# Starting the first values half an exponential early, and the row-sum count as a full-width product, in a fused attention and SwiGLU kernel

## The chip, the cores and the metric

The kernel runs on one core of one Trainium2 chip. The metric is the device time of one execution in microseconds (us), of the slowest core, here the only one.

Short names: PE is TensorE with its products, PEld its loads of weights, ACT is ScalarE, DVE is VectorE, POOL is GpSimd, SP is SyncE, which only issues transfers. L487 is line 487 of the kernel in question; the changed kernel's lines are 3 higher from the first edit on.

## The reference, cut to what matters

```python
# x [1, 2048, 640], 32 heads of 192, caches of 2048 keys, F = 1536, all bf16
xn = _layernorm(x)
q = (xn @ wq) per head                       # [32, 2048, 192]
scores = q @ k_cache.T * (192 ** -0.5)
p = softmax(scores);  o = p @ v_cache
s = o (heads joined) @ wo
g = silu(silu(xn @ w1) * (xn @ w3) @ w2)
return x + s * g
```

## The kernel before

The attention is a stream of 1024 steps (head h, block of 512 queries qb, pair of key tiles p). A step n has three pieces: *scores n* (six products into a PSUM tile `st2`, of which there are two), *exponential n* on ACT (into `pT2`, which frees the score tile), *values n* (16 products that read `pT2`). On PE, scores run two steps ahead of values. The exponential takes no maximum; instead the kernel keeps the reciprocals of the row sums and at the end counts the rows in which these are in range. If the count is not full, an exact attention is run; with these inputs it never is. `project` and `project0` make the queries from the normalised rows `xnT` and `xnS`, a copy with the halves exchanged; `P` is 128.

```python
def emit_scores(h, qb, p):
    st2 = ps_st.tile([P, 1024], F32, tag="st2", name="st2")     # two buffers
    # rounds: pairs of products, rows 0-63 into columns 0:512, rows 64-127 into 512:1024
    # [cut: the first two steps have two full-height products in place of two rounds]
    for r, (ka, qa, kb, qb2) in enumerate(rounds):
        nc.tensor.matmul(st2[:, 0:512], lhsT=ka, rhs=qa, ...)
        nc.tensor.matmul(st2[:, 512:1024], lhsT=kb, rhs=qb2, ...)
    pT2 = pp.tile([P, 1024], BF16, tag="pT2", name="pT2")
    nc.scalar.activation(out=pT2[:], in_=st2[:], func=ACT.Exp, scale=att_scale)
    return pT2

# [cut: head_start(): loads, layernorm of the first 512 rows, scores(0), scores(1)]

for n, (h, qb, p) in enumerate(stream):
    # [cut: project(h + 1, qb) or ffn_open(qb) at p == 0]
    if h == 0 and qb == 0 and p == 3:
        project(1, 0)
    if h == 0 and qb + 1 < NQB and p == (5 if qb == 0 else 4):
        project0(qb + 1)
    scores(n + 2)
    values(n)
    # [cut: end of a block, SwiGLU pieces, layernorm of later rows: first_head()]
```

`project(1, 0)` makes head 1's queries for the first 512 rows. It uses the two row halves of the array at the same time, and the products that pair with the other half read `xnS`, a copy of the normalised rows `xnT` with the halves exchanged. That copy is made by two transfers that SP issues at about 11 and 12 us. `project0(1)` makes head 0's queries for rows 512 to 1023, and half of these rows reach `xnT` by two transposing transfers (`ln_turn_dma`), which SP issues at about 18 to 20 us. `P` is 128; `DC` is 5, the 640 columns of x in pieces of 128.

```python
def swap_halves(g):
    nc.sync.dma_start(out=xnS[0:64, :, qs], in_=xnT[64:P, :, qs])
    nc.sync.dma_start(out=xnS[64:P, :, qs], in_=xnT[0:64, :, qs])

def ln_turn_dma(g, i):
    nc.sync.dma_start_transpose(out=xnT[:, :, q0:q0 + P], in_=xns.pop((g, i))[:])

def two_products(W, qs):                       # of project(h, qb)
    for j in range(2 * DC):
        for r in range(2):
            rows = slice(r * 64, (r + 1) * 64)
            xs = xnT if j % 2 == r else xnS
            nc.tensor.matmul(ps[:, r * 512:(r + 1) * 512], lhsT=W[rows, j, :], rhs=xs[rows, j // 2, qs], ...)

def project0(qb):
    for half in range(2):
        for c in range(DC):
            nc.tensor.matmul(ps[:, half * 512:(half + 1) * 512], lhsT=W[:, half * DC + c, :], rhs=xnT[:, c, qs], ...)
```

The count stands in the output stage, after the fifth of 16 output tiles (24 products each):

```python
    if i == 4:
        cnt = ps_st.tile([P, 1024], F32, tag="st2", name="cnt")
        nc.tensor.matmul(cnt[0:2, 0:2], lhsT=ones[:], rhs=okb[:], start=True, stop=True)   # ones: [P, 2]
```

Of the kernel before, what the change touches and what calls it, by code (L numbers as in the profile page):

```python
# [8 lines left out]
ACT = mybir.ActivationFunctionType  # L9
ALU = mybir.AluOpType  # L10
AX = mybir.AxisListType
BF16 = mybir.dt.bfloat16
# [3 lines left out]
P = 128  # L16
# [112 lines left out]
def _kernel_impl(  # L129
# [12 lines left out]
    nc = tc.nc  # L142
# [16 lines left out]
    att_scale = float(DH) ** -0.5  # L159
# [243 lines left out]
    def project0(qb):  # L403
        W = loads[0]["W"]
        qAB, qC = q_tiles(0, qb)
        qs = slice(qb * 512, (qb + 1) * 512)
        ps = ps_st.tile([P, 1024], F32, tag="st2", name="ps0")
        for half in range(2):
            for c in range(DC):
                nc.tensor.matmul(ps[:, half * 512:(half + 1) * 512], lhsT=W[:, half * DC + c, :], rhs=xnT[:, c, qs],  # L410
                                 start=(c == 0), stop=(c == DC - 1))
        cast_pair(qAB, ps)
        nc.vector.tensor_copy(out=qC[64:P, 0, :], in_=qAB[0][0:64, :])
        nc.vector.tensor_copy(out=qC[0:64, 0, :], in_=qAB[0][64:P, :])
        nc.vector.tensor_copy(out=qC[0:64, 1, :], in_=qAB[1][64:P, :])
# [18 lines left out]
    def project(h, qb):  # L434
        qAB, qC = q_tiles(h, qb)
        cast_pair(qAB, two_products(loads[h]["W"], slice(qb * 512, (qb + 1) * 512)))
        move_q(qAB, qC, 0)
        move_q(qAB, qC, 1)
# [3 lines left out]
    def ffn_open(qb):  # L442

        pairs[qb] = [qp.tile([P, 512], BF16, tag=t, name=t) for t in ("qA", "qB")]
        cast_pair(pairs[qb], two_products(wrest["wf"], slice(qb * 512, (qb + 1) * 512)))
# [9 lines left out]
    def swiglu(h, qb):  # L455

        m = h // 2
        qs = slice(qb * 512, (qb + 1) * 512)
        z = qtiles[h, qb][0][1][0:PGW, :]
        r0 = (m % 2) * PGW  # L460
        hid = hT[r0:r0 + PGW, m // 2, qs]
        if h % 2 == 0:
            t = hbp.tile([P, 512], BF16, tag="pt", name="pt")
            nc.scalar.activation(out=t[0:PGW, :], in_=z, func=ACT.Tanh, scale=0.5)  # L464
            nc.vector.scalar_tensor_tensor(out=hid, in0=t[0:PGW, :], scalar=1.0, in1=z, op0=ALU.add, op1=ALU.mult)  # L465
        else:
            nc.vector.scalar_tensor_tensor(out=hid, in0=hid, scalar=0.5, in1=z, op0=ALU.mult, op1=ALU.mult)
# [3 lines left out]
    def emit_scores(h, qb, p):  # L471


        KW = loads[h]["KW"]
        (qA, qB), qC = qtiles[h, qb]
        ks = slice(p * P, (p + 1) * P)
        st2 = ps_st.tile([P, 1024], F32, tag="st2", name="st2")
        rounds = [(KW[0:64, 0, ks], qA[0:64, :], KW[64:P, 1, ks], qC[64:P, 0, :]),
                  (KW[0:64, 3, ks], qC[0:64, 0, :], KW[64:P, 4, ks], qA[64:P, :]),
                  (KW[0:64, 1, ks], qC[0:64, 1, :], KW[64:P, 2, ks], qB[64:P, :])]  # L480
        if (h, qb) == (0, 0) and p < 2:
            rounds = rounds[2:]
            nc.tensor.matmul(st2[:, 0:512], lhsT=KW[:, 0, ks], rhs=qA[:], start=True, stop=False)
            nc.tensor.matmul(st2[:, 512:1024], lhsT=KW[:, 4, ks], rhs=qA[:], start=True, stop=False)
        nr = len(rounds)
        for r, (ka, qa, kb, qb2) in enumerate(rounds):
            nc.tensor.matmul(st2[:, 0:512], lhsT=ka, rhs=qa, start=r == 0 and nr == 3, stop=r == nr - 1)  # L487
            nc.tensor.matmul(st2[:, 512:1024], lhsT=kb, rhs=qb2, start=r == 0 and nr == 3, stop=r == nr - 1)  # L488
        pT2 = pp.tile([P, 1024], BF16, tag="pT2", name="pT2")
        nc.scalar.activation(out=pT2[:], in_=st2[:], func=ACT.Exp, scale=att_scale)  # L490
        return pT2

    exps = {}
# [5 lines left out]
    def scores(n):  # L499
        if n < len(stream):  # L500
            exps[n] = emit_scores(*stream[n])

    def values(n):

        h, qb, p = stream[n]
        if p == 0:
            for r in range(2):
                obanks[r] = ps_o.tile([P, 1024], F32, tag=f"ob{r}", name=f"obank{r}")
        vt = loads[h]["vt"]
        pT2 = exps.pop(n)  # L510
        for t in range(2):
            for j in range(4):
                start = p == 0 and t == 0 and j % 2 == 0
                stop = p == NPAIR - 1 and t == 1 and j % 2 == 1
                for r in range(2):
                    nc.tensor.matmul(obanks[r][:, j * 256:j * 256 + DH + 1],  # L516
                                     lhsT=pT2[r * 64:(r + 1) * 64, t * 512 + j * P:t * 512 + (j + 1) * P],
                                     rhs=vt[r * 64:(r + 1) * 64, 2 * p + t, 0:DH + 1], start=start, stop=stop)
        if p < NPAIR - 1:
            return  # L520
        if h % HG == 0 and qb == 0:
            ostages[0] = stp.tile([P, NQT, HG * DH], BF16, tag="ostage", name="ostage")
        ov = [obanks[r][:].rearrange("p (j w) -> p j w", j=4)[:, :, 0:DH + 1] for r in range(2)]
        osum = osp.tile([P, 4, DH + 1], F32, tag="osum", name="osum")
        nc.vector.tensor_copy(out=osum[:], in_=ov[0])  # L525
        nc.vector.tensor_tensor(out=osum[:], in0=osum[:], in1=ov[1], op=ALU.add)  # L526
        osums[0] = osum
# [96 lines left out]
    def finish_block(n):  # L624
        h, qb, _ = stream[n]
        finish_values(h, qb)
        loads_after(h, qb)
# [26 lines left out]
    for n, (h, qb, p) in enumerate(stream):  # L654
        if p == 0 and n > 0:
            if h + 1 < H:
                project(h + 1, qb)
            else:
                ffn_open(qb)
        if h == 0 and qb == 0 and p == 3:  # L660
            project(1, 0)
        if h == 0 and qb + 1 < NQB and p == (5 if qb == 0 else 4):
            project0(qb + 1)
        scores(n + 2)
        values(n)
        if p == 0 and n > 0:
            finish_block(n - 1)
        if p == (5 if h == 0 else 2) and h < 2 * NPIG:
            swiglu(h, qb)
        if p == 4 and h + 1 == H:  # L670
            ffn_close(qb)
        if h == 0:
            first_head(qb, p)
# [6 lines left out]
    fsb = main.enter_context(tc.tile_pool(name="fsb", bufs=2))  # L680
# [15 lines left out]
    for qb in range(NQB):  # L696
        qs = slice(qb * 512, (qb + 1) * 512)
        for fl in range(FL2 // P):
            ps = pools[(qb * (FL2 // P) + fl) % 2].tile([P, 1024], F32, tag="st2", name="ps_gu")
            for r, w in enumerate((wrest["w1"], wrest["w3"])):  # L700
                for c in range(DC):
                    nc.tensor.matmul(ps[:, r * 512:(r + 1) * 512], lhsT=w[:, c, fl * P:(fl + 1) * P], rhs=xnT[:, c, qs],  # L702
                                     start=(c == 0), stop=(c == DC - 1))
# [10 lines left out]
    okb = fsb.tile([P, 2], BF16, tag="okb", name="okb")  # L714
    nc.vector.tensor_scalar(out=okb[:, 0:1], in0=ends[:, 0:1], scalar1=RL_MAX, scalar2=None, op0=ALU.is_lt)
    nc.vector.tensor_scalar(out=okb[:, 1:2], in0=ends[:, 1:2], scalar1=RL_MIN, scalar2=None, op0=ALU.is_gt)
    ones = fsb.tile([P, 2], BF16, tag="ones", name="ones")
    nc.vector.memset(ones[:], 1.0)


    def g_of(i):
        return hT[:, 0:DC, i * P:(i + 1) * P]

    for i in range(NQT):
        ps = pools[i % 2].tile([P, 1024], F32, tag="st2", name="ps_f")
        for fc in range(FC):
            for b, (c0, c1) in enumerate(DP):
                nc.tensor.matmul(ps[:, b * 512:b * 512 + c1 - c0], lhsT=hT[:, fc, i * P:(i + 1) * P],  # L728
                                 rhs=w2_sb[:, fc, c0:c1], start=(fc == 0), stop=(fc == FC - 1))
        for b, (c0, c1) in enumerate(DP):  # L730
            t = fsb.tile([P, 512], BF16, tag="ft", name="ft")
            pv = ps[:, b * 512:b * 512 + c1 - c0]
            nc.scalar.activation(out=t[:, 0:c1 - c0], in_=pv, func=ACT.Tanh, scale=0.5)
            nc.vector.scalar_tensor_tensor(out=g_of(i)[:, c0 // P:c1 // P, :],
                                           in0=t[:, 0:c1 - c0].rearrange("p (a w) -> p a w", w=P), scalar=1.0,
                                           in1=pv.rearrange("p (a w) -> p a w", w=P), op0=ALU.add, op1=ALU.mult)
        if i == 4:
            cnt = ps_st.tile([P, 1024], F32, tag="st2", name="cnt")
            nc.tensor.matmul(cnt[0:2, 0:2], lhsT=ones[:], rhs=okb[:], start=True, stop=True)
            tot = fsb.tile([1, 1], F32, tag="tot", name="tot")  # L740
            nc.vector.tensor_reduce(out=tot[:], in_=cnt[0:1, 0:2], axis=AX.X, op=ALU.add)
            nc.vector.tensor_copy(out=flag[:], in_=tot[:])
# [65 lines left out]
```

## Time and profile before

| | before |
|---|---|
| time, median of the first 3 runs | 1939.36 us (1938.64 to 1939.67) |
| span of the profiled run | 1936.7 us |
| PE busy | 1927.1 us |
| PE busy between 16.10 and 1660 us | 1643.64 of 1643.90 us |

The head of the profile page of the kernel before, and its chain of waits (what released the last work, followed back from the end):

```profile
PE 1927.1 (100%) x27273; PEld 1317.2 (68%) x27281; DVE 654.4 (34%) x997; ACT 1181.5 (61%) x1278; POOL 282.1 (15%) x501
...
PE 99%; DVE 0%; DMA 0%; ACT 0%; issue 0%
```

PE is busy all the time and nearly the whole chain is PE. So a change is worth something only if it takes work or a wait off PE. The list of PE's waits (line and tile, what it waited for, us in total, times, longest):

```profile
PE pk L569 <- POOL ident_bf masks.py:199: 2.8, 1, 2.8
PE pst L354 <- DVE xn L346: 0.8, 1, 0.8
PE st L487 <- ACT pT L490: 0.3, 1, 0.3
PE st L483 <- DVE qA L393: 0.2, 1, 0.2
```

Four waits, all in the first 16 us. The change is after the third. Here it is in the timeline (start in us, duration in us, engine, line, operation, out<-in, form; in brackets the idle time before it and what ended it), ACT first and then PE:

```profile
14.38 1.94 ACT L490 ACTIVATE pT<-st 128x1024 bf16<-128x1024 f32 x2
```

```profile
14.78 0.39 PE L487 MATMUL st<-qC,KW 64*128 64x512 bf16 x1
14.79 0.39 PE L488 MATMUL st<-qB,KW 64*128 64x512 bf16 x1
15.45 0.37 PE L487 MATMUL st<-qA,KW 64*128 64x512 bf16 x1 [0.28 <-ACT pT L490]
...
16.77 0.38 PE L487 MATMUL st<-qA,KW 64*128 64x512 bf16 x1
```

Scores 1 end with the two products at 14.78, and scores 3 begin at 16.77. Scores 2 are next in order and need the tile that the first exponential reads, so they start at 15.45, when it is done. The bracket says 0.28 us of idle time because a product is counted as busy for 0.38 us from its start. Products normally start 0.216 us apart here, so from start to start (14.785 to 15.454 in the trace) 0.45 us is lost. The Trainium skill ("Perfetto Trace Analysis", section "Tensor Engine Instruction (MATMUL, LD_WEIGHTS)") gives the reason to count from start to start: the end that the profiler gives for a product is estimated from its size, not measured.

The count, in the timeline of PE:

```profile
1684.81 2.17 PE L728 MATMUL ps_f<-w_all,hT 128*128 128x256 bf16 x15
1686.91 0.16 PE L739 MATMUL cnt<-okb,ones 128*2 128x2 bf16 x1
1687.01 0.45 PE L728 MATMUL ps_f<-w_all,hT 128*128 128x384 bf16 x2
```

The count has the form `128*2`, a tile of the array 2 columns wide, among products of the form `128*128`. In the trace the product ahead of it starts at 1686.707 and the one behind it at 1687.006, 299 ns later; that first product alone takes 109 ns.

### The profile page before, as it was taken

The page shows a single profiled execution, that of the slowest core. Times are in us where ns is not written, and L with a number is a line of the kernel's source. Part 1 is how long each engine was busy: PE and PEld are TensorE (multiplying, and loading weights), DVE is VectorE, ACT ScalarE, POOL GpSimd, SP SyncE. Part 2 cuts the span into 40 slices and gives each one's busy share as a digit, 9 for nine tenths or more (in the row PEclk, how much of TensorE's full clock was granted, in tenths as well). Part 3 has the DMA queues.
Part 4 walks back from the last instruction along what each step waited for, and adds up shares of the span by engine and source line. Part 5 has one row for each costly group of instructions (what it writes and reads, how often), then busy time and mean ns, then how long its engine had stood idle before and what let it go on. Part 6 is the DMA issues. An engine that isn't in the chain of part 4 may idle for free.

```text
span 1936.7 us, 59668 instructions
## 1 busy us (share of the span) xinstructions
PE 1927.1 (100%) x27273; PEld 1317.2 (68%) x27281; DVE 654.4 (34%) x997; ACT 1181.5 (61%) x1278; POOL 282.1 (15%) x501
## 2 busy tenths in 40 slices
PE   9999999999999999999999999999999999999998
PEld 6666666666666666666666666666666666577776
DVE  7333333333333333333333333333333334521111
ACT  6677676767676767776777777677767677210000
POOL 3111111111111111111111111111111110000000
PEclk9999999999999999999999999999999999999999
DMA  8643433323333434363434343434334220937772
GB/s 181 129 101 67 98 68 85 84 59 92 58 90 61 99 64 97 68 162 68 101 66 100 69 101 69 101 64 100 69 68 97 60 67 2 249 79 137 152 153 60
DMA packets 394643, 178.98 MB, mean 92 GB/s; under 512 B 341616, under 2 KB 382832, under 8 KB 394384
## 3 DMA queue, kind: packets, MB, share of 16 engines
q1 hardware_dynamic: 371136, 125.32, 31.5%
q0 software_dynamic: 19472, 45.71, 10.1%
q8 instruction: 215, 3.52, 0.8%
q10 hardware_dynamic: 3776, 4.06, 0.6%
q14 instruction: 44, 0.36, 0.1%
HBM read 52.82 MB, written 27.79 MB: 42 GB/s over the span
## 4 chain that ended last, share of the span: by engine, by line
PE 99%; DVE 0%; DMA 0%; ACT 0%; issue 0%
PE obank L516 35%; PE st L487 34%; PE ps L424 14%; PE ps_s L111 11%; PE ps_f L728 3%; PE ps_gu L702 1%; PE st L488 1%; PE ps L410 0%; DMA x_all<-in_A_x_dram 0%; DVE stats L316 0%; PE ps L391 0%; PE pst L354 0%; PE pk L271 0%; ACT pT L490 0%; DVE mv L317 0%
## 5 line engine op out<-in xcount | busy, mean ns | idle before, releaser
L490 ACT ACTIVATE pT<-st 128x1024 bf16<-128x1024 f32 x1024 | 1047.4, 1023 | 248.8 <-PE st L488 233.2
L516 PEld LDWEIGHTS <-pT 64*128 64x128 bf16 x16384 | 711.6, 94 | 242.0 <-ACT pT L490 0.2
L516 PE MATMUL obank<-vt,pT 64*128 64x193 bf16 x16384 | 849.6, 243 | 0.0
L487 PE MATMUL st<-qC,KW 64*128 64x512 bf16 x2046 | 605.6, 376 | 0.1
L525 DVE COPY osum<-obank 128x772 f32<-128x772 f32 x128 | 123.1, 962 | 786.9 <-PE obank L516 786.9
L488 PE MATMUL st<-qB,KW 64*128 64x512 bf16 x1024 | 385.0, 376 | 0.0
L487 PE MATMUL st<-qA,KW 64*128 64x512 bf16 x1022 | 384.3, 376 | 0.3 <-ACT pT L490 0.3
L488 PE MATMUL st<-qC,KW 64*128 64x512 bf16 x1022 | 384.3, 376 | 0.0
L488 PE MATMUL st<-qA,KW 64*128 64x512 bf16 x1022 | 384.3, 376 | 0.0
L487 PEld LDWEIGHTS <-KW 64*128 64x128 bf16 x3068 | 278.4, 94 | 153.3 <-issue 2.1
L424 PE MATMUL ps<-xnT,W 64*128 64x512 bf16 x1280 | 297.3, 376 | 0.0
L424 PE MATMUL ps<-xnS,W 64*128 64x512 bf16 x1280 | 296.2, 376 | 0.0
L488 PEld LDWEIGHTS <-KW 64*128 64x128 bf16 x3068 | 278.5, 94 | 0.8 <-issue 0.6
L377 POOL DMA_DIRECT2D qC<-qA x124 | 65.4, 528 | 1283.4 <-DVE rl_all L532 1268.5
L430 ACT CAST qB<-ps 128x512 bf16<-128x512 f32 x131 | 76.8, 586 | 228.2 <-PE ps L424 222.7
L111 PE MATMUL ps_s<-wo_sb,oT 128*128 128x384 bf16 (+3 forms) x1535 | 208.7, 299 | 0.1
L424 PEld LDWEIGHTS <-W 64*128 64x128 bf16 x2560 | 123.6, 94 | 120.7
L111 PEld LDWEIGHTS <-oT 128*128 128x128 bf16 x1536 | 148.4, 98 | 60.4
L526 DVE TENSOR_TENSOR osum<-osum,obank 128x772 f32<-128x772 f32 x128 | 122.7, 959 | 13.4
L533 DVE TENSOR_TENSOR ostage<-osum,rl_all 128x768 bf16<-128x768 f32 x128 | 122.6, 958 | 6.2 <-DMA o_scr<-ostage 1.9
L465 DVE SCALAR_TENSOR_TENSOR hT<-pt,qB 64x512 bf16<-64x512 bf16 x64 | 43.8, 684 | 197.6 <-ACT pt L464 197.6
L429 DVE CAST qA<-ps 128x512 bf16<-128x512 f32 x131 | 90.6, 692 | 25.3 <-PE ps L410 7.2
(84 smaller groups left out, 620.8 us busy)
## 6 DMA issues: line engine op xcount, KB each, us to landing
o_scr<-ostage SPq DMA_DIRECT2D x16, 1536.0 KB, 10.6
vt<-in_A_v_cache_dram SPq DMA_DIRECT2D x63, 384.0 KB, 5.9
qC<-qA POOLq DMA_DIRECT2D x248, 64.0 KB, 2.0
qC<-qB POOLq DMA_DIRECT2D x124, 64.0 KB, 2.3
wo_sb<-in_A_wo_dram POOLq DMA_DIRECT2D x1, 7680.0 KB, 37.8
W<-in_A_wq_dram POOLq DMA_DIRECT2D x32, 160.0 KB, 3.6
W<-in_B_w_dram POOLq DMA_DIRECT2D x32, 80.0 KB, 3.3
W<-in_A_wq_dram POOLq DMA_DIRECT2D x32, 80.0 KB, 2.9
```

Source lines behind the costliest of these rows:

```text
L111: nc.tensor.matmul(ps[:, 0:w], lhsT=oT[:, k, :], rhs=wo_sb[:, k, c0:c1], start=(k == 0), stop=(k == OC - 1))
L377: nc.gpsimd.dma_start(out=qC[0:64, half, :], in_=qAB[half][64:P, :])
L424: nc.tensor.matmul(ps[:, r * 512:(r + 1) * 512], lhsT=W[rows, j, :], rhs=xs[rows, j // 2, qs], start=(j == 0), stop=(j == 2 * DC - 1))
L429: a = nc.vector.tensor_copy(out=qAB[0][:], in_=ps[:, 0:512])
L430: b = nc.scalar.copy(out=qAB[1][:], in_=ps[:, 512:1024])
L487: nc.tensor.matmul(st2[:, 0:512], lhsT=ka, rhs=qa, start=r == 0 and nr == 3, stop=r == nr - 1)
L488: nc.tensor.matmul(st2[:, 512:1024], lhsT=kb, rhs=qb2, start=r == 0 and nr == 3, stop=r == nr - 1)
L490: nc.scalar.activation(out=pT2[:], in_=st2[:], func=ACT.Exp, scale=att_scale)
L516: nc.tensor.matmul(obanks[r][:, j * 256:j * 256 + DH + 1], lhsT=pT2[r * 64:(r + 1) * 64, t * 512 + j * P:t * 512 + (j + 1) * P], rhs=vt[r ...
L525: nc.vector.tensor_copy(out=osum[:], in_=ov[0])
L526: nc.vector.tensor_tensor(out=osum[:], in0=osum[:], in1=ov[1], op=ALU.add)
L533: nc.vector.tensor_tensor(out=ostage[:, qb * 4:qb * 4 + 4, hg * DH:(hg + 1) * DH], in0=osum[:, :, 0:DH], in1=rl.unsqueeze(2).to_broadcast( ...
```

## The change

The intent: give PE something to do while the first exponential runs, by computing it in two halves of 512 columns and putting values 0, whose first eight products need only the first half, ahead of scores 2; and take the odd array shape out of the output stage by making the count 128 columns wide (all of its rows are the same count, one is read as before).

```diff
@@ emit_scores
-        nc.scalar.activation(out=pT2[:], in_=st2[:], func=ACT.Exp, scale=att_scale)
+        parts = 2 if (h, qb, p) == (0, 0, 0) else 1
+        w = 1024 // parts
+        for c in range(parts):
+            nc.scalar.activation(out=pT2[:, c * w:(c + 1) * w], in_=st2[:, c * w:(c + 1) * w], func=ACT.Exp, scale=att_scale)
@@ the stream
-        scores(n + 2)
-        values(n)
+        for step in (values, scores) if n == 0 else (scores, values):
+            step(n + 2 if step is scores else n)
@@ the count
-    ones = fsb.tile([P, 2], BF16, tag="ones", name="ones")
+    ones = fsb.tile([P, P], BF16, tag="ones", name="ones")
@@
-            nc.tensor.matmul(cnt[0:2, 0:2], lhsT=ones[:], rhs=okb[:], start=True, stop=True)
+            nc.tensor.matmul(cnt[:, 0:2], lhsT=ones[:], rhs=okb[:], start=True, stop=True)
```

## The prediction

> **What bounds the kernel.** TensorE. The page gives PE 1927.1 us busy of 1936.7, and the chain of waits is 99% PE. Busy time by window shows 1643.64 us of PE in the 1643.90 us from 16.10 to 1660; the granted clock is 1.00. The list of waits has four for PE: 2.8 us before the warm-up products, 0.8 us for the layernorm, 0.3 and 0.2 us at the first scores. The change touches one small wait and one isolated product.
>
> **Part 1, the start.** In the timeline, scores 1 finish issuing at 14.785 us. Scores 2 then wait for a score buffer that the first exponential (14.379 to 15.403) frees; PE goes on at 15.454. Start to start that is 669 ns where 216 is normal: 0.45 us lost. Now values 0 come first, and their first eight products need only half the exponential.
>
> - A 128x1024 exponential takes 1.024 us; starts follow each other by 0.92 when inputs are ready. The Trainium skill ("ScalarE: Activation LUTs", What ACT_TABLE_LOAD costs) gives 0.833 ns per element and 93 ns overlap of neighbours, which the trace fits. Estimate for a half: 1024 - 427 = 0.60 us.
> - First half ready about 14.98, values 0 start about 15.03. Eight products take 0.33 us, to 15.37.
> - Second half ends about 15.47, so PE waits again, 0.15 us, and runs the other eight to about 15.86. Scores 2 take 0.65 us, to 16.50. Before, both were done at 16.765.
> - Gain here: 0.27 us. Given back later? The second exponential ends about 16.39; scores 3 need it at 16.50. The third starts about 16.7 instead of 16.31 and ends about 17.75; scores 4 need its buffer about 17.81. Both just in time, then PE-bound. I take 0.2 us (0.05 to 0.35).
> - The values' first half must have landed by 15.03: issued by 7.1 us, 6.6 us to landing in the DMA view, so about 14.
>
> **Part 2, the count.** Its product runs in a 128*2 mode amid 128*128 ones. From the product before it to the one after, the timeline shows 299 ns (1686.707 to 1687.006), where that product alone needs 109. The Trainium skill ("TensorEngine Tiling (Array Packing)", Key Properties) says that a change of tiling mode drains the engine; the two late starts (about 0.09 us each) agree. At full width there is no change of mode, only an overlapped load and a two-column product, estimated at 30 to 60 ns: gain about 0.14 us, all on PE's critical path. Setting the wider ones tile is on DVE, 34% busy: free.
>
> **Elsewhere** the order on every engine is unchanged; ACT has one instruction more.
>
> **Predicted time.** 1939.36 - 0.2 - 0.14 = 1939.0 us; 8 in 10 between 1937.4 and 1940.4, a range set by the spread from run to run (1 us among three). Faster by over 2%: 0.01; within 2%: 0.98; slower: 0.01.
>
> **What would show it.** In the waits of PE: values on the exponential twice (0.2 to 0.3 us together or each) in place of scores once; two 128x512 exponentials of about 0.60 us; products about 0.2 us earlier after the first values block, with a steady stream of equal length; the count as 128*128, followed by the next product within 60 ns.
>
> **What would make it wrong.** Values 0 waiting for the values load; the third exponential late for scores 4, returning the gain; the wider count waiting for something that the narrow one hid; a run-to-run shift above 1 us, which would swamp all of it.

## The result, and the profile after

| | before | changed |
|---|---|---|
| time, median of 6 runs each | 1938.84 us (1938.13 to 1939.67) | 1938.31 us (1937.68 to 1938.64) |
| ratio | | 0.9997, 95% interval 0.9984 to 1.001: the same |
| span of the profiled run | 1936.7 us | 1936.4 us |

A ratio is the mean time of one kernel's runs over that of the other's of the same rounds, so it is not quite the ratio of the medians quoted. The result is correct. The interval is some 5 us wide and the effects looked for are tenths of a microsecond, so the timed runs can only say "the same". What follows rests on the traces, in which a step of PE's stream repeats to a few nanoseconds.

The same places in the profile of the changed kernel. The page:

```profile
PE 1926.6 (99%) x27273; PEld 1315.6 (68%) x27281; DVE 654.6 (34%) x997; ACT 1180.0 (61%) x1279; POOL 282.5 (15%) x501
...
PE 99%; DVE 1%; DMA 0%; ACT 0%; issue 0%; DVEq 0%; ACTq 0%
```

PE's waits, and the wait of its weight loads that the change brought:

```profile
PE pk L572 <- POOL ident_bf masks.py:199: 2.8, 1, 2.8
PE pst L354 <- DVE xn L346: 0.9, 1, 0.9
PE st L483 <- DVE qA L393: 0.2, 1, 0.2
```

```profile
PEld L519 <- ACT pT L493: 0.6, 3, 0.2
```

The wait of scores 2 is gone from the first list. It is not gone altogether: values 0 still wait for each half, but the wait now stands with the loads of weights (0.6 us in all; before, this group waited for 0.2 us), because for values the exponential's result is the weight. ACT and PE there:

```profile
14.08 2.00 ACT L493 ACTIVATE pT<-st 128x512 bf16<-128x512 f32 x3
```

```profile
14.49 0.39 PE L487 MATMUL st<-qC,KW 64*128 64x512 bf16 x1
...
14.74 0.99 PE L519 MATMUL obank<-vt,pT 64*128 64x193 bf16 x16
15.57 0.38 PE L487 MATMUL st<-qA,KW 64*128 64x512 bf16 x1
...
16.21 0.38 PE L487 MATMUL st<-qA,KW 64*128 64x512 bf16 x1
```

Values 0 start at 14.74, 0.25 us after the last product of scores 1, in place of the 0.67 us before. They are spread over 0.99 us, as their ninth product waits for the second half (the trace has 14.997, then 15.224). Scores 2 start at 15.57 and scores 3 at 16.21. From the last product of scores 1 to the first of scores 3 it is 1.726 us; before it was 1.980. That is a gain of 0.25 us, where 0.27 was forecast at this point.

And the count:

```profile
1686.00 0.71 PE L731 MATMUL ps_f<-w_all,hT 128*128 128x384 bf16 x4
1686.55 0.17 PE L742 MATMUL cnt<-okb,ones 128*128 128x2 bf16 x1
1686.57 0.59 PE L731 MATMUL ps_f<-w_all,hT 128*128 128x384 bf16 x3
```

It has the form `128*128`, and the next product starts 28 ns after it. From the product ahead of it to the product behind it: 137 ns in place of 299; with the next start counted too, 299 in place of 472, so 0.173 us saved.

Both local effects are as forecast. Yet the attention as a whole is not shorter. From the first product of scores 0 to the start of the last exponential, 13.398 to 1642.752 before and 13.101 to 1642.479 after:

```profile
13.40 0.38 PE L483 MATMUL st<-qA,KW 128*128 128x512 bf16 x1 [0.16 <-DVE qA L393]
```

```profile
1642.75 1.02 ACT L490 ACTIVATE pT<-st 128x1024 bf16<-128x1024 f32 x1
```

```profile
13.10 0.38 PE L483 MATMUL st<-qA,KW 128*128 128x512 bf16 x1 [0.16 <-DVE qA L393]
```

```profile
1642.48 1.01 ACT L493 ACTIVATE pT<-st 128x1024 bf16<-128x1024 f32 x1
```

That is 1629.354 us before and 1629.378 us after. (That everything stands 0.3 us earlier in the second trace is the chance of when the first inputs arrived, the first load of x landing at 3.86 us before and at 3.56 us after; both kernels do the same until scores 0.) So within the attention the 0.25 us was given back. Where? In the chain of waits between 18 and 26 us, `project(1, 0)` and `project0(1)` (its pieces: start us, length us, what):

```profile
19.57 2.16 PE ps L424 x20
...
25.13 0.32 PE ps L410
```

```profile
19.01 2.36 PE ps L424 x20
...
24.76 0.07 issue
24.84 0.38 PE ps L410
```

The 20 products of `project(1, 0)` take 2.36 us instead of 2.16. And ahead of `project0(1)` stands a new piece of 0.07 us in which PE waits for something that the view cannot name ("issue"). The timeline of PE shows the first:

```profile
19.39 0.38 PE L424 MATMUL ps<-xnT,W 64*128 64x512 bf16 x1
19.41 0.38 PE L424 MATMUL ps<-xnS,W 64*128 64x512 bf16 x1
```

```profile
18.84 0.38 PE L424 MATMUL ps<-xnT,W 64*128 64x512 bf16 x1
19.05 0.39 PE L424 MATMUL ps<-xnS,W 64*128 64x512 bf16 x2
```

Before, the two row halves of the array start `project(1, 0)` together, 0.02 us apart. After, the upper half starts at 18.84 with a product on `xnT`, and the lower half, whose first product reads the exchanged copy `xnS`, starts 0.205 us later. The halves then run that far apart until the form changes from `64*128` to `128*128` at the turning products (22.61 us), where the leading half must wait. So a lag of 0.205 us in one half cost 0.200 us: the turning products start 9.509 us after scores 0 here, and 9.309 us after them in `after_again` below, which has the same order and no lag. The time to landing of the second transfer into `xnS`, from its issue at about 11.6 to 11.9 us (L365), in each of the two runs:

```profile
DMA to landing us min/median/max: 7.1/7.1/7.1
```

```profile
DMA to landing us min/median/max: 7.4/7.4/7.4
```

In the changed kernel that landing is at 19.006 us in the trace and the product that reads it starts at 19.048.

The same for the two turned tiles (L360), before and after. The later of the two, on which `project0(1)` depends, took 5.1 us to land before (to 24.83, read at 25.06) and 5.3 us after (to 24.70, read at 24.84). In these lines of both tiles together it is the maximum before and the minimum after:

```profile
DMA to landing us min/median/max: 4.3/4.7/5.1
```

```profile
DMA to landing us min/median/max: 5.3/5.7/6.0
```

So the theory, called A below: the gain is real at the first exponential, but the next things that PE needs are two transfers, whose landing has nothing to do with PE's progress. PE arrives earlier and waits. Rivals: (B) the new order itself leaves the row halves apart, or a later wait takes the gain; (C) this one profile is chance and the gain is there as a rule.

### The profile page after: what moved, and what is told of

It reads as the page before. It is cut to its first block, busy times and chain, and to the rows that moved or that the text cites. A ratio compares the mean times of both kernels' runs of the same rounds, so it can differ in the third digit from the quotient of the medians. Undisturbed runs are those within 1.5% of the kernel's fastest.

```text
span 1936.4 us, 59669 instructions
## 1 busy us (share of the span) xinstructions
PE 1926.6 (99%) x27273; PEld 1315.6 (68%) x27281; DVE 654.6 (34%) x997; ACT 1180.0 (61%) x1279; POOL 282.5 (15%) x501
## 4 chain that ended last, share of the span: by engine, by line
PE 99%; DVE 1%; DMA 0%; ACT 0%; issue 0%; DVEq 0%; ACTq 0%
PE obank L519 35%; PE st L487 34%; PE ps L424 14%; PE ps_s L111 11%; PE ps_f L731 3%; PE ps_gu L705 1%; PE st L488 1%; PE ps L410 0%; DVE stats L316 0%; DMA x_all<-in_A_x_dram 0%; PE ps L391 0%; PE pst L354 0%; PE pk L271 0%; DVE xn L346 0%; ACT pT L493 0%
## 5 line engine op out<-in xcount | busy, mean ns | idle before, releaser
L493 ACT ACTIVATE pT<-st 128x1024 bf16<-128x1024 f32 (+1 forms) x1025 | 1046.1, 1021 | 250.2 <-PE st L488 234.0
```

Of the source, the lines that this page charges most:

```text
L493: nc.scalar.activation(out=pT2[:, c * w:(c + 1) * w], in_=st2[:, c * w:(c + 1) * w], func=ACT.Exp, scale=att_scale)
```

## The experiments

All twelve gave a correct result. Each has one profile; some were also timed in five rounds. Two measures recur. *Hand-over* is from the start of the last product of scores 1 to the first of scores 3. *Attention* is from the start of the first product of scores 0 to that of the last exponential. Times "after scores 0" count from that same first product, which takes the chance of the input's arrival out.

### Part 1 alone, part 2 alone

`part1_only` is the changed kernel with the count as before. `part2_only` is the kernel before with the wide count. No other line differs from the diff above.

> Measures used in all expectations: HAND-OVER = start of the last product of scores 1 to start of the first product of scores 3 (before 1.98 us, changed kernel 1.73 us); ATTENTION = start of the first product of scores 0 to start of the last exponential (before 1629.35, changed 1629.38). Theory A (landings): the change gains 0.25 us at the hand-over and gives it back within 10 us, because the next work waits for transfers of the activations whose landing is not earlier: HAND-OVER 1.73, ATTENTION within 0.1 us of before, timed 0.0 to 0.15 us faster than before. Rival C (the profile was chance and the 0.25 us is kept): ATTENTION 0.2 to 0.3 us shorter in this second sample, timed 0.25 us faster.

> From the product before the count to the product after it: 0.137 us as in the changed kernel, against 0.299 before; with the next product counted, 0.17 us less. ATTENTION as before (1629.3 to 1629.5). Timed 0.17 us faster, which the spread of the runs may hide. If the count were worth nothing, the output stage would be as long as before.

Measured, part 1 alone: hand-over 1.726 us, attention 1629.390 us (before: 1629.354). The swapped copy landed 5.93 us after scores 0, and its first reader started at 5.97; `project0(1)` started at 11.75 (before: 11.67). Timed 1938.51 us against 1938.44 for before, medians of 5 and 9 runs. So a second sample shows the whole gain given back again; rival C was wrong for this one.

Measured, part 2 alone: 138 ns around the count (299 before), and the stretch from the first tanh of the output tiles to the last takes 50.098 us against 50.274. Timed 1938.64 against 1938.44. The 0.17 us is plain in the trace and invisible in the timed runs. The expectation for its attention failed: 1629.659 us, 0.3 longer than before, though the start is that of the kernel before. In this execution the turned tiles landed late, 11.86 us after scores 0, and `project0(1)` started at 12.00. So this wait also befalls the unchanged order when a landing is late enough, which B does not explain.

### The order alone, the division alone

```diff
# order_only: changed kernel, narrow count, and
-        parts = 2 if (h, qb, p) == (0, 0, 0) else 1
+        parts = 1
# split_only: changed kernel, narrow count, and
-        for step in (values, scores) if n == 0 else (scores, values):
+        for step in (scores, values):
```

> Undivided exponential, values 0 ahead of scores 2. PE now waits for the same exponential with other work: HAND-OVER 1.98 us as before (no gain), so the whole gain of part 1 needs the division. If the order alone helped, HAND-OVER would be 1.75 to 1.85.

> Divided exponential, old order. Scores 2 wait for both halves, which end 0.06 us later than the undivided one (two of 0.60 us, overlapping by 0.10): HAND-OVER 2.04 us, 0.06 worse than before.

Measured: hand-over 1.996 us with the order alone and 2.040 us with the division alone, against 1.980 before. Neither half of part 1 gains without the other: with the order alone PE waits for the same exponential, with the division alone the two halves end 0.06 us later. Single times 1938.41 and 1938.52 us.

### Work put ahead of the two landings

If A holds, the gain must stay when PE has other work until the transfers land. `hide_both` does that: in `project` the products that read `xnT` come first, and in `project0(1)` the columns that PE itself turned come first. About 1.1 us of work then stands ahead of each landing.

```diff
-        for j in range(2 * DC):
+        for s in range(2 * DC):
             for r in range(2):
                 rows = slice(r * 64, (r + 1) * 64)
+                j = 2 * s + r if s < DC else 2 * (s - DC) + 1 - r
                 xs = xnT if j % 2 == r else xnS
@@ project0
+        parts = ((256, 512), (0, 256)) if qb == 1 else ((0, 512),)
+        for a, b in parts:
-        for half in range(2):
-            for c in range(DC):
+            for half in range(2):
+                for c in range(DC):
# [cut: the product on columns a:b, start on the first of a bank, stop on the last]
```

`hide_only` has the same two moves in the kernel before; `hide_swap` and `hide_turn` have only the first and only the second in the changed kernel.

> The changed kernel, with the products of project(1,0) that read the swapped copy (landing about 19.0 to 19.4) put after the ones that do not, and the products of project0(1) that read the tiles turned by DMA (landing about 24.8 to 25.4) put after the ones turned on TensorE: about 1.1 us of work ahead of each landing. Results stay correct. Theory A (part 1's gain is eaten by these two landings): no lag between the row groups at project(1,0), no wait before project0(1) (0.18 us from the last product before it, not 0.31), ATTENTION 1629.10 us, 0.25 below before; whole kernel about 0.43 us faster than before. Rival B (the new order itself leaves the row groups apart, or the loss lies in a later wait, such as that for the casts at the tenth scores): ATTENTION stays at 1629.35 to 1629.40.

> The kernel before with the same two moves and neither part of the change. Theory A: before waits for nothing there except when a landing is late, so ATTENTION is 1629.3 to 1629.4 (as before's 1629.35); timed within 0.1 us of before. If the moves alone gained 0.25 us, then hide_both would not show that part 1 is worth anything.

> The changed kernel with only the first move (swapped copy). Theory A: no lag at project(1,0) and the turning products start about 0.25 us earlier against scores 0 than before (9.33 instead of 9.58), but project0(1) waits for its landing, about 0.3 us or more, and starts about 11.7 us after scores 0 as before: ATTENTION 1629.35 to 1629.40.

> The changed kernel with only the second move (tiles turned by DMA). Theory A: the lag of about 0.2 us at project(1,0) stays and costs 0.18 us, project0(1) waits for nothing: ATTENTION about 1629.28, 0.07 below before.

| run | attention | turning products, after scores 0 | `project0(1)`, after scores 0 |
|---|---|---|---|
| before | 1629.354 | 9.580 | 11.665 |
| hide_only | 1629.346 | 9.581 | 11.666 |
| hide_turn | 1629.336 | 9.570 | 11.655 |
| hide_both | 1629.083 | 9.309 | 11.394 |
| hide_swap | 1629.049 | 9.309 | 11.394 |

`hide_both` and `hide_only` came out as A says: the moves alone are worth nothing, the moves with the change 0.27 us. `hide_turn` nearly did: the lag at `project(1, 0)` was 0.27 us and not 0.2, as the copy landed at 5.97, so nothing of the gain was left rather than 0.07. `hide_swap` did not: it was to wait at `project0(1)` and kept everything instead. The trace says why: in that execution the tiles landed at 11.15 us after scores 0, where 11.26 would have been in time. But in `hide_both` both landings were early as well (5.34 and 11.03), so its profile did not test the moves. More samples were needed.

### The same kernels again

`hide_again` and `hide_third` are `hide_both` once more, `after_again` is the changed kernel once more.

> The same kernel as hide_both, whose one profile fell on an execution in which both landings were early (swapped copy 5.34 us after scores 0, turned tiles 11.03), so that it could not tell whether the moves protect the gain. Over all ten profiles so far the two landings range over 5.29 to 6.03 and 11.03 to 11.86. Theory A: whatever the landings are here, ATTENTION is 1629.05 to 1629.10, project0(1) starts 11.39 us after scores 0 and the turning products 9.31 us after them. Against that: if it is 1629.3 or more with landings later than 5.75 or 11.35, the moves protect nothing. Timed about 0.4 us faster than before.

> The changed kernel once more. Theory A: the start of the first product that reads the swapped copy is the later of its place in order (5.74 us after scores 0) and the landing plus about 0.04; project0(1) starts at the later of its place and the landing plus about 0.13. With late landings (over 5.75 or 11.45) ATTENTION 1629.3 to 1629.4; with early ones (below 5.5 and 11.2) it would be 1629.05 to 1629.10, the gain kept. Timed 0.2 to 0.5 us faster than before, with hide_again at or below it.

> A third profile of hide_both, for the same reason: ATTENTION 1629.05 to 1629.10 at any landing, if theory A holds.

`after_again` met the earliest landings of all. Its timeline shows no lag at `project(1, 0)`, the chain of waits has 2.16 us for it again, and the second transfer into `xnS` took 6.6 us to land:

```profile
19.13 0.38 PE L424 MATMUL ps<-xnT,W 64*128 64x512 bf16 x1
19.13 0.59 PE L424 MATMUL ps<-xnS,W 64*128 64x512 bf16 x2
```

```profile
19.29 2.16 PE ps L424 x20
```

```profile
DMA to landing us min/median/max: 6.6/6.6/6.6
```

Its attention is 1629.052 us: the gain is kept whole. `hide_third` met landings as late as those of the first profile of the changed kernel (7.4 us from issue, as there), and kept the gain all the same, 1629.104 us. Its chain of waits and the time to landing:

```profile
19.18 2.16 PE ps L428 x20
```

```profile
DMA to landing us min/median/max: 7.4/7.4/7.4
```

All fourteen profiles, all in us after scores 0. "Landed" is the issue of the later transfer plus its time to landing, from the trace:

| run | swapped copy landed | its first reader started | turned tiles landed | `project0(1)` started | attention |
|---|---|---|---|---|---|
| before | 5.61 | 6.02 | 11.43 | 11.67 | 1629.354 |
| order_only | 5.29 | 6.02 | 11.10 | 11.67 | 1629.355 |
| split_only | 5.81 | 6.08 | 11.59 | 11.73 | 1629.381 |
| part2_only | 6.03 | 6.07 | 11.86 | 12.00 | 1629.659 |
| hide_only | 5.96 | (moved) | 11.67 | 11.67 (moved) | 1629.346 |
| changed | 5.91 | 5.95 | 11.60 | 11.74 | 1629.378 |
| part1_only | 5.93 | 5.97 | 11.62 | 11.75 | 1629.390 |
| hide_turn | 5.97 | 6.01 | 11.65 | 11.66 (moved) | 1629.336 |
| hide_swap | 5.44 | (moved) | 11.15 | 11.39 | 1629.049 |
| after_again | 5.02 | 5.74 | 10.89 | 11.39 | 1629.052 |
| hide_both | 5.34 | (moved) | 11.03 | 11.39 (moved) | 1629.083 |
| hide_again | 5.72 | (moved) | 11.47 | 11.40 (moved) | 1629.072 |
| hide_third | 5.91 | (moved) | 11.56 | 11.40 (moved) | 1629.104 |
| count_mixed | 7.89 | 7.94 | 11.89 | 13.58 | 1631.260 |

In every unmoved row the reader of the swapped copy starts at the later of two times: its own place in order (6.02 in the old order, 6.08 with the division alone, 5.74 with part 1), and the landing plus 0.04. `project0(1)` does the same with its place (11.67, 11.73 and 11.39, moved back by whatever lag the swapped copy left, to 13.58 in count_mixed) and the landing plus 0.135. In the first profile of the changed kernel both took a part: the lag moved the place from 11.39 to 11.60, and the landing the start to 11.74. `hide_again` and `hide_third` started it at 11.40 with tiles that landed at 11.47 and 11.56. Attention then follows `project0(1)` by 1617.6 to 1617.7 us in all rows. So B is out: with the same order and early landings the gain stays, and with late landings and the readers moved it stays too. C is out as a rule: in 10 of the 14 executions a landing was late enough to take at least some of the gain from an unmoved kernel (over 5.70 or 11.26). What stays open is why the landings differ by up to 1 us between executions of the same code.

The record narrows that question. The experiments ran on three chips, and the swapped copy's landing spread on each of them (5.29 to 6.03, 5.34 to 5.97, 5.02 to 7.89), so it is not a difference of chips. Nor are the two landings two separate chances: in all but count_mixed the turned tiles landed 5.65 to 5.87 us after the swapped copy, so the two move together. From 11.9 to 19 us, while the copy was under way, the packets of SP's queue took 93 to 99% of the time of the 16 DMA engines (six traces looked at), and loads of 640 and 384 KB that SP issued after the copy shared them. Whether the copy would land earlier if these loads were issued later was not tried.

The timed expectations of this group can't be judged at this spread, and one missed: the changed kernel was to be 0.2 to 0.5 us faster than before in `after_again` and its median was 0.25 us slower, with a ratio of 1.0 and an interval of 0.9986 to 1.0013.

As a kernel to keep, `hide_both` had the lowest medians of those timed in five rounds: 1938.08 and 1938.10 us in two sets of 5 runs, against 1938.68 and 1938.69 for before (9 runs each). The changed kernel in the second of these sets had 1938.94. The ratios are 0.9996 and 0.9998, with intervals that contain 1, so by the timed runs this too is "the same"; the traces say 0.27 us in the attention and 0.17 us at the count.

### The price of a narrow count, many times over

`count_mixed` puts a count ahead of each of the 12 pairs of products of every output tile, narrow in the first eight tiles and wide in the last eight.

```diff
+        cnt = ps_st.tile([P, 1024], F32, tag="st2", name="cnt")
+        wd = 2 if i < 8 else P
         for fc in range(FC):
+            nc.tensor.matmul(cnt[0:wd, 0:2], lhsT=ones[:, 0:wd], rhs=okb[:], start=True, stop=True)
# [and without the single count of tile 4; ones is 128 columns wide]
```

> The kernel before, with a count product ahead of each of the 12 pairs of products of every output tile: two columns of ones in tiles 0 to 7, 128 columns in tiles 8 to 15 (a correct result still). From the first tanh of one tile to that of the next: 3.26 us without any count. If each narrow count costs the 0.20 us read from the one before (change of tiling mode and back), 5.66 us; each wide one 0.03 us, so 3.60 us. If the cost were that of any extra product or of its load of weights, both halves would be equally long. Whole kernel about 8 x 2.4 + 8 x 0.34 = 22 us slower than before.

The first tanh of successive output tiles, in a narrow tile and in a wide one (ACT):

```profile
1690.08 0.49 ACT L736 ACTIVATE ft<-ps_f 128x384 bf16<-128x384 f32 x1 [4.25 <-PE ps_f L731]
...
1695.76 0.49 ACT L736 ACTIVATE ft<-ps_f 128x384 bf16<-128x384 f32 x1 [4.19 <-PE ps_f L731]
```

```profile
1742.09 0.49 ACT L736 ACTIVATE ft<-ps_f 128x384 bf16<-128x384 f32 x1 [2.07 <-PE ps_f L731]
...
1745.65 0.49 ACT L736 ACTIVATE ft<-ps_f 128x384 bf16<-128x384 f32 x1 [2.07 <-PE ps_f L731]
```

5.68 us and 3.56 us per tile, as expected (5.66 and 3.60), against 3.26 in the kernel before. Twelve narrow counts cost 2.42 us, so 0.20 us each; twelve wide ones 0.30 us, so 0.025 each. The load of the weights and the product itself are there in both; the form is what differs. Which part of the narrow form costs the time (a drain at the change of form, or its own load of weights) these runs do not separate.

The whole kernel took 1978.9 us, 40 us more than before and not 22. The expected 22 us are there; the sum left out two things. The first is the start: in this execution the swapped copy landed 2 us late, which made the attention 1.9 us longer. The second is the clock (columns: stretch, its length, busy time of each engine, granted clock, DMA):

```profile
1672.00:1684.34 12.34, 8.69 (x40) 2.54 (x38) 3.24 (x8) 0.60 (x1) 0.00 (x0) 0.72 1.04 347
...
1690.08:1707.12 17.04, 16.95 (x108) 6.91 (x108) 2.92 (x6) 2.62 (x6) 0.00 (x0) 1.00 1.15 225
1707.12:1734.87 27.75, 25.74 (x110) 7.68 (x110) 3.12 (x8) 2.62 (x7) 0.00 (x0) 0.57 0.02 3
1734.87:1738.50 3.63, 3.63 (x38) 2.66 (x37) 0.97 (x2) 0.87 (x2) 0.00 (x0) 1.00 0.02 5
```

PE idled for 3.6 us before the first count (for the tile of ones) and for 2.1 us at 1707 (for a buffer), and both times the granted clock fell to one half soon after. The first time it was back after 6.8 us, while narrow counts ran; the second time it stayed at one half for 23.9 us, until 1734.86 us, which is when the wide tiles begin (1734.56). Three tiles lay in that stretch and took 8.9 to 10.0 us each, 10.7 us more than at full clock and without the wait; with the 6.2 us that the first wait and the first drop cost ahead of the first tanh, and the 1.9 of the start, that makes 18.8 us, where 18.2 were to be explained (40.2 less 22). The Trainium skill ("TensorE: Matmul & The Clock Gate", "Part 1: The HAM clock gate") describes a gate that halves the clock after an idle window of about 3.4 us and opens it again when PE is busy. The first idle time is longer than that window; the second, 2.1 us, is shorter, so the page does not explain the second drop. (In the trace the four changes of the clock lie 6.827, 27.307 and 23.893 us apart, which is 2, 8 and 7 times 3.413 us.) Whether narrow counts kept the gate from opening is not shown: the wide ones began 0.3 us before it opened, but the first time it opened amid narrow ones. It does not touch the per-tile figures above, which come from stretches at clock 1.00.

## Why the prediction was right or wrong

The time was forecast as 1939.0 us (1937.4 to 1940.4) and "within 2%" with a chance of 0.98; it was 1938.31, with 1938.84 for before. Right, but easily so: the range came from the spread of the runs. The steps are the better test.

- *PE bounds the kernel, and only small waits are to be had*: right.
- *Half exponentials of 0.60 us, values 0 at about 15.03, their second half at 15.52, scores 2 at 15.86*: right. The trace has 0.597 and 0.592 us. Moved by the 0.297 us that the second trace is early, it has 15.03, 15.52 and 15.86. The Trainium skill's figures for ScalarE ("ScalarE: Activation LUTs", section "What ACT_TABLE_LOAD costs") of 0.833 ns per element and 93 ns overlap fit the difference of 427 ns between the two sizes and the 0.10 us by which the halves overlap.
- *Gain of 0.27 us at scores 3*: 0.254 measured.
- *Both exponentials just in time*: right. The third ends at 17.44 (17.74 when moved, 17.75 forecast) and scores 4 start at 17.53 (17.83; 17.81 forecast).
- *"Both just in time, then PE-bound. I take 0.2 us"*: this step failed. The prediction asked whether the gain would be given back and looked only at ACT. The next limits were two transfers, 4 and 10 us on from values 0. In the profiled execution of before, the swapped copy landed 0.36 us and the turned tiles 0.1 us before they would have been waited for, so of a gain of 0.27 us the turned tiles alone could take back 0.17. The term forecast as a gain of 0.2 us measured a loss of 0.02 in the first profile of the changed kernel, a loss of 0.04 in `part1_only` and a gain of 0.30 in `after_again` (attention against that of before), by the chance of the landings. The check that the prediction did make of a transfer, that of the values' first half, was right: it landed at 12.74 us, and values 0 started at 14.74.
- *The count saves about 0.14 us; the wide one costs 30 to 60 ns*: the mechanism was right and the size low. It saved 0.173 us, since the wide count costs 28 ns and the narrow one delays the following start by another 10 ns. The Trainium skill ("TensorEngine Tiling (Array Packing)", "Key Properties") says that a change of tiling mode drains the engine; that the narrow form costs 0.20 us and the wide 0.025 in otherwise equal loops agrees with it.
- *"Products about 0.2 us earlier after the first values block, with a steady stream of equal length"*: not so in the first profile, for the reason above; so in `after_again`.
- *"In the waits of PE: values on the exponential twice"*: they stand with the weight loads, 0.6 us in 3 waits where before it was 0.2, and PE's own list is shorter. A reader of that list alone would have believed the wait gone.

Of the 0.53 us by which the medians differ, the count gives 0.17. That the 0.53 comes near the 0.34 forecast is luck, for the rest is not established: the changed kernel's second set of runs was 0.25 us slower than before, and the only trace-proven gain of part 1 is one that comes and goes with the landings.

## What to carry to other kernels

When a wait on a critical engine is shortened, list what that engine needs next from any source, with the time at which it arrives, and include transfers issued long before: those that landed just in time are the next wait, and they do not move. Put work that does not need a transfer's data ahead of work that does, even inside one accumulation; here it cost nothing (`hide_only`, 1629.346 us of attention against 1629.354) and kept the gain at every landing that it met. And for effects below the spread of the timed runs, count intervals between starts in several traces; one trace is one throw of the dice.

## What the Trainium skill lacked or had wrong

- "TensorEngine Tiling (Array Packing)": it says that a change of mode drains the engine, with no figure. Here a single two-column product between full-width ones costs 0.20 us (299 ns from neighbour to neighbour, 10 ns more on the next start), a full-width one 0.025 to 0.028 us. How much of the difference is the drain is not separated.
- "TensorE: Matmul & The Clock Gate", Part 3: it has row tiles that run at the same time, but not that one row half can fall behind by a late operand and stay behind, here by 0.205 us for 3.6 us, until a change of form makes the other wait for it. (Starts stayed in program order: when the operand was 1.94 us late, in count_mixed, the other half's second product waited too and started 6 ns after the late one.)
- "DMA: Bandwidth & Descriptors": it gives a fixed cost of about 2 us per transfer, fitted to transfers issued from GpSimd (those here are issued by SP), and not how far the landing of one and the same transfer spreads under load. The same two transfers, issued at the same place in the code, landed 5.0 to 6.0 us and 10.9 to 11.9 us after the first scores in thirteen executions, and the first of them at 7.9 in the fourteenth.
- "TensorE: Matmul & The Clock Gate", Part 1: the clock halved after 2.1 us of idle time, less than the window stated, and stayed so for 23.9 us while the records show PE busy with alternating narrow and full-width products. The page's table lets activity raise the clock again after about one window; a caveat on it tells of a gate seen stuck, but at a quarter of the clock.
